# Transposing keys as fp32 words of two bf16, and a query projection in row form, in a decode step that streams 162 MB

## The chip, the cores and the metric

The kernel runs on 1 core of one Trainium2 chip. The metric is the device time of one execution in microseconds (us), given as the median of several runs. The *span* is the time from the first to the last instruction that the profile shows. It is shorter than the device time: 390.4 us of 393.2 us in the profiled run of the kernel before.

Engine names: PE multiplies matrices, PEld is PE's weight load, DVE, ACT and POOL are the vector, scalar and general engines, SP only starts loads here.

## The reference, cut to what matters

One token of one sequence goes through attention over a cache, and through a gated MLP, and a gate mixes the two. Everything is bf16.

```python
# x [1,1,1024]; k_cache, v_cache [1,4,65536,128]; wq [1024,4096]; wo [4096,1024]
g = sigmoid((x * gate_w).sum(-1))
q = x @ wq                                    # 32 query heads of 128, 8 to each key head
p = softmax(q @ k.T * 128 ** -0.5)            # over 65536 keys
a = (p @ v).reshape(1, 1, 4096) @ wo
b = gmlp(x, w_in, w_sp, b_sp, w_out)
return g * a + (1 - g) * b
```

## The kernel before

All large operands pass through one ring of five 4 MB slots. There are 41 loads: 2 of wq, 16 pairs of key units, 16 pairs of value units, 2 of w_in, 1 of w_out, 4 of wo. SP starts load n when the last PE instruction that reads load n−5 has ended. This is the only link from the speed of PE back to the speed of the loads.

```python
# issue(): SP starts load n into slot n % NS (NS = 5); the operation has to wait
# for all readers of the slot. done(key): the last key of load n was used, start n + 5.
P("SP", f, w=[("slot", s)], dma="s%d" % s)
...
# gate: needs gate_w, and is recorded ahead of the query projection
P("DVE", lambda e: e.tensor_tensor(z2[:, 0:KC], xT, gw, ALU.mult), r=["xT", "gw"], w=["z2"])
...
# query projection, column form: 256 matmuls of one column
for k in range(2):
    for h in range(HQ):
        ins = e.matmul(pf(OB)[:, h:h + 1], sl[:, WQ_N * k + 128 * h:WQ_N * k + 128 * (h + 1)],
                       xT[:, 2 * i + k:2 * i + k + 1], ...)
```

A *unit* is 8192 keys of one key head. Keys lie in rows; this kernel's product with the queries reads them in columns, so a unit takes 64 transposes of 128x128, in 8 batches into PSUM, each batch copied out by DVE (5 of 8) or ACT (3 of 8), and then 16 score matmuls.

```python
def tr(e, b=b, pb=pb):                        # one batch of k_piece
    for t in range(8):
        ins = e.transpose(pbf(pb)[:, 128 * t:128 * (t + 1)],
                          sl[:, 128 * (8 * b + t):128 * (8 * b + t + 1)], idb)
...
def f(e):                                     # s_piece, after every two batches
    for cg in range(4):
        src = ktb(first + cg // 2)[:, 512 * (cg % 2):512 * (cg % 2 + 1)]
        ins = e.matmul(pf(SCB)[32 * cg:32 * (cg + 1), :],
                       qpad[:, 128 * g + 32 * j:128 * g + 32 * (j + 1)], src, ...)
```

A matmul or a transpose of bf16 is two PE instructions, a weight load and a multiply: the 2048 key transposes are 2048 of each on the page.

Of the kernel before, what the change touches and what calls it, by code (L numbers as in the profile page):

```python
# [137 lines left out]
def bass_gated_mix__gqa_block_cached__mixer_gmlp__decode_kernel(  # L138
# [28 lines left out]
    NS = 5  # L167
    SLOT = 16384
    NB = TILES // 8
    NKTS = 6  # L170
    NSC = 10
    QW = DO // 4
    SCALE = 1.0 / math.sqrt(Dh)
# [13 lines left out]
    for name, n in [  # L187
        ("RING", NS * SLOT), ("KT", NKTS * 1024), ("SC", NSC * 1024), ("PSB", 1024), ("PTSB", 1024),
        ("QPAD", G * 128), ("IDB", 128), ("IDF", 256), ("BM", 256), ("ONES", 256), ("SEL", 16 * 32),
        ("M16", 32), ("M8", 16), ("M32", 64), ("MQ", 32), ("OT", 256), ("XT", KC), ("GW", KC), ("WB", 2), ("MAXC", 2 * G * NU), ("LP", 2 * G * NU),  # L190
        ("COLS", 2 * 64), ("DM", 32), ("OSB", 1024), ("OSC", 512), ("OV", OC), ("Z", 2 * 28), ("Z2", 2 * 28),
        ("ZG", 2 * 28), ("ZE", 2 * 28), ("YB", FC), ("BROW", 2 * QW), ("OROW", QW),
    ]:
        region(name, n)
# [3 lines left out]
    def ab(name, n, o=0):  # L198
        return arena[:, OFF[name] + o:OFF[name] + o + n]

    def af(name, n, o=0):
        return arena[:, OFF[name] + 2 * o:OFF[name] + 2 * (o + n)].bitcast(F32)
# [11 lines left out]
    maxc, lp, colt = af("MAXC", G * NU), af("LP", G * NU), af("COLS", 64)  # L214
    zc, z2, zg, ze = af("Z", 28), af("Z2", 28), af("ZG", 28), af("ZE", 28)
    yb, ovec, orow, brow = ab("YB", FC), ab("OV", OC), ab("OROW", QW), af("BROW", QW)
    osb, osc, dm = af("OSB", 512), ab("OSC", 512), af("DM", 16)
    col = lambda i: colt[:, i:i + 1]
    (C_GS, C_GE, C_G1, C_G, C_OMG, C_MU, C_V, C_S0, C_R0, C_S1, C_R1, C_AL, C_BE, C_T) = range(14)
    C_G4 = 16  # L220
# [1 line left out]
    def gcol(g, i):  # L222
        return col(C_G4 + 11 * g + i)
# [20 lines left out]
    def B(i):  # L244
        return ("bank", i)
# [7 lines left out]
    P("DVE", lambda e: e.memset(ones, 1.0), w=["ones"])  # L253
    P("DVE", lambda e: e.memset(brow, 0.0), w=["brow"])
    P("DVE", lambda e: e.memset(pf(MB), 0.0), w=[B(MB)])


    def small(dst, src, key):
# [106 lines left out]
      r=["m32"], w=["sel"])  # L365
    P("DVE", lambda e: e.tensor_reduce(mq, vw(idf, 0, [[1, 16], [16, 8]]), AXX, ALU.add), r=["idf"], w=["mq"])


    P("DVE", lambda e: e.tensor_tensor(z2[:, 0:KC], xT, gw, ALU.mult), r=["xT", "gw"], w=["z2"])  # L369
    P("DVE", lambda e: e.tensor_reduce(col(C_GS), z2[:, 0:KC], AXX, ALU.add), r=["z2"], w=["gs"])  # L370
# [6 lines left out]
      r=["g"], w=["omg"])  # L377


    for i in range(4):  # L380
        sl, key = use(("wq", i))

        def f(e, i=i, sl=sl):
            for k in range(2):
                for h in range(HQ):
                    ins = e.matmul(pf(OB)[:, h:h + 1], sl[:, WQ_N * k + 128 * h:WQ_N * k + 128 * (h + 1)],  # L386
                                   xT[:, 2 * i + k:2 * i + k + 1], start=(i == 0 and k == 0 and h == 0),
                                   stop=(i == 3 and k == 1), skip_group_check=True)
            return ins
        P("PE", f, r=["xT", key], w=[B(OB)])  # L390
        done(("wq", i))
    for g in range(G):
        P("DVE", lambda e, g=g: e.tensor_copy(vw(qpad, 128 * g, [[40, 4], [1, 8]]),
                                              vw(pf(OB), 8 * g, [[0, 4], [1, 8]])),
          r=[B(OB)], w=["qpad"])


    nbatch = [0]
    pend = []

    def k_piece(n, j):
        sl, key = use(("k", n))
        first = nbatch[0]
        for b in (2 * j, 2 * j + 1):
            i = nbatch[0]
            nbatch[0] += 1
            pb = KTB[i % 4]

            def tr(e, b=b, pb=pb):
                for t in range(8):  # L410
                    ins = e.transpose(pbf(pb)[:, 128 * t:128 * (t + 1)],  # L411
                                      sl[:, 128 * (8 * b + t):128 * (8 * b + t + 1)], idb)
                return ins
            P("PE", tr, r=["idb", key], w=[B(pb)])
            if b in (2, 5, 7):
                P("ACT", lambda e, i=i, pb=pb: e.activation(ktb(i), pbf(pb), ACTF.Copy),  # L416
                  w=[("kt", i % NKTS), B(pb)])
            else:
                P("DVE", lambda e, i=i, pb=pb: e.tensor_copy(ktb(i), pbf(pb)), w=[("kt", i % NKTS), B(pb)])  # L419
        if j == 3:  # L420
            done(("k", n))
        pend.append((n, j, first))

    def s_piece():
        if not pend:
            return
        n, j, first = pend.pop(0)
        g, u = KV[n]

        def f(e):  # L430
            for cg in range(4):
                src = ktb(first + cg // 2)[:, 512 * (cg % 2):512 * (cg % 2 + 1)]
                ins = e.matmul(pf(SCB)[32 * cg:32 * (cg + 1), :], qpad[:, 128 * g + 32 * j:128 * g + 32 * (j + 1)], src,  # L433
                               start=(j == 0), stop=(j == 3), tile_position=(0, 32 * cg), skip_group_check=True)
            return ins
        P("PE", f, r=["qpad", ("kt", first % NKTS), ("kt", (first + 1) % NKTS)], w=[B(SCB)])
        if j == 3:
            P("DVE", lambda e: e.tensor_scalar(scs(n), pf(SCB), 0.0, None, op0=ALU.add, op1=ALU.max,  # L438
                                               accum_out=maxc[:, n:n + 1]), w=[("sc", n % NSC), ("mx", n), B(SCB)])
            if u == NU - 1:  # L440
                max_piece(g)
# [29 lines left out]
    def pv_piece(n):  # L471
        g, u = KV[n]
        sl, key = use(("v", n))

        def f(e):
            for xi in range(4):
                for cg in range(4):
                    ins = e.matmul(pf(OB)[32 * cg:32 * (cg + 1), :],  # L478
                                   ptsb(n)[:, 128 * xi + 32 * cg:128 * xi + 32 * (cg + 1)],
                                   vw(sl, 128 * (4 * cg + xi), [[2048, 4], [1, 128]]),  # L480
                                   start=(u == 0 and xi == 0), stop=(u == NU - 1 and xi == 3),
                                   tile_position=(0, 32 * cg), skip_group_check=True)
            return ins
        P("PE", f, r=[("ptsb", n % 2), key], w=[B(OB)])
        done(("v", n))
        if u == NU - 1:
            out_piece(g)

    def out_piece(g):
        P("DVE", lambda e: e.tensor_copy(osb, pf(OB)), w=["osb", B(OB)])  # L490
        P("DVE", lambda e: e.tensor_reduce(gcol(g, K_L), lp[:, NU * g:NU * (g + 1)], AXX, ALU.add),
          r=[("lp", NU * g + u) for u in range(NU)], w=[("l", g)])
        P("DVE", lambda e: e.tensor_tensor(gcol(g, K_LW), gcol(g, K_L), gcol(g, K_W), ALU.mult),
# [4 lines left out]
        P("DVE", lambda e: e.scalar_tensor_tensor(gcol(g, K_F), gcol(g, K_RL), gcol(g, K_W), col(C_G),  # L498
                                                  op0=ALU.mult, op1=ALU.mult),
          r=[("rl", g), ("w", g), "g"], w=[("f", g)])  # L500
        P("DVE", lambda e: e.tensor_scalar(osc, osb, gcol(g, K_F), None, op0=ALU.mult),
          r=["osb", ("f", g)], w=["osc"])

        def f(e):
            for c in range(4):
# [86 lines left out]
    for si, (k, v, aux) in enumerate(steps):  # L592
# [4 lines left out]
            start_exp(v)  # L597
        for j in range(4):
            if k is not None:
                k_piece(k, j)  # L600
                s_piece() if len(pend) > 1 else None
            if j == 1 and v is not None:
                pt_piece(v)
            if j == 2 and nxt is not None and (k is not None or not pend):
                start_exp(nxt)
            if j == 3 and v is not None:
                pv_piece(v)
# [53 lines left out]
```

## Time and profile before

| | before |
|---|---|
| device time, median of 3 runs | 392.74 us (392.17 to 393.21) |
| span of the profiled run | 390.4 us (other runs of this kernel: up to 392.9) |
| bytes loaded | 162.01 MB |
| PE busy, and its mean granted clock | 274.1 us, 0.850 |
| PE instructions | 3902 multiplies and 3902 weight loads |

These are lines of the page of the kernel before. The first three give the span, the busy time of each engine, and the rate of the loads in 40 slices of 9.76 us; `q1` is the queue of the loads, `q8` and `q14` are queues of instruction fetches (packets, MB, share of the time of 16 DMA engines); then come the shares of the chain of work that ended last, and two costly groups (busy us, mean ns of one | idle time just before, and what ended it).

```profile
span 390.4 us, 8502 instructions
...
PE 274.1 (70%) x3902; PEld 194.6 (50%) x3902; DVE 160.2 (41%) x347; ACT 124.4 (32%) x171; POOL 1.5 (0%) x8
...
GB/s 322 430 430 437 418 412 441 426 428 425 411 405 431 433 426 431 428 431 428 427 431 428 428 431 430 425 435 435 428 431 433 428 426 431 433 431 421 416 415 96
...
q1 hardware_dynamic: 5912, 162.01, 97.1%
q8 instruction: 30, 0.49, 0.5%
...
q14 instruction: 4, 0.03, 0.0%
...
DMA 55%; PE 36%; DVE 6%; issue 1%; ACT 1%; ACTq 0%; DVEq 0%
...
L411 PE MATMUL pb<-arena 128*128 128x128 bf16 x2048 | 153.6, 235 | 31.7 <-DMA arena<-in_A_k_cache_dram 31.7
L411 PEld LDWEIGHTS pb<-arena 128*128 128x128 bf16 x2048 | 131.9, 106 | 60.1 <-DMA arena<-in_A_k_cache_dram 34.7
```

The loads run at about 430 GB/s almost throughout and their queue fills 97.1% of the time of 16 DMA engines, so the loads set the time. PE, busy 70% of the time, spends it mostly on the 2048 key transposes.

The next lines are the timeline of SP, cut to three loads: the time of an issue, its duration, the engine and the line, and what is loaded. An issue shows when a slot came free. The first two slots are those of wq, the third is a key slot.

```profile
44.99 0.33 SPq L338 DMA_DIRECT2D arena<-in_B_w_in_dram  x1
50.67 0.33 SPq L338 DMA_DIRECT2D arena<-in_A_k_cache_dram  x1
...
106.72 0.33 SPq L338 DMA_DIRECT2D arena<-in_A_k_cache_dram  x1
```

The following stretches show busy time per engine with counts in brackets, granted clock, share of busy DMA and the rate. The first shows a dip to 344 GB/s. The issue at 106.72 us above came when the queue was running dry. (The rate of a stretch counts a packet whole where it starts, so stretches of 2 us scatter by tens of GB/s; this one is of 6 us.) The last three stretches are the end of the stream.

```profile
core 0: us, PE busy (x) PEld busy (x) DVE busy (x) ACT busy (x) POOL busy (x), PEclk, DMA share, GB/s
106.00:112.00 6.00, 5.79 (x91) 4.39 (x89) 4.00 (x8) 3.47 (x4) 0.00 (x0) 1.00 0.88 344
380.00:382.00 2.00, 1.01 (x32) 0.67 (x32) 0.00 (x0) 0.00 (x0) 0.00 (x0) 1.00 0.60 254
382.00:384.00 2.00, 0.04 (x4) 0.00 (x0) 0.00 (x0) 0.00 (x0) 0.00 (x0) 0.54 0.52 221
384.00:386.00 2.00, 0.05 (x4) 0.08 (x8) 0.00 (x0) 0.00 (x0) 0.00 (x0) 0.50 0.17 74
```

The end of the timeline before shows the matmuls of the last wo load and the addition that follows. They start at 385.95 us.

```profile
385.95 1.88 PE L621 MATMUL pb<-arena 128*1 128x256 bf16 x32 [3.91 <-DMA arena<-in_A_wo_dram]
387.88 0.42 DVE L627 TENSOR_TENSOR arena<-pb,arena 97x256 bf16<-97x256 f32 x1 [12.56 <-PE pb L621]
```

### The profile page before, as it was taken

Reading aid. Unit: us, or ns where it says so; the run is one execution under the profiler, and the core shown is the slowest. Engines: PE = TensorE matmul, PEld = TensorE weight load, DVE = VectorE, ACT = ScalarE, POOL = GpSimd, SP = SyncE. Lnnn points to the kernel's source line nnn. Section 1 sums busy time; section 2 is a strip of 40 time slices with the busy share of each in tenths; the row PEclk is TensorE's granted clock in tenths of the full one; section 3 lists DMA queues with packets and bytes.
Section 4 is the critical chain, followed back from the end, with each engine's and each line's share of the span. In section 5 each row is a group of like instructions: output and inputs, shape, how many; then the busy total and the mean of one; then the engine's idle time right before and its main releaser. Section 6 shows DMA issues by size and latency. Waiting matters only on the chain.

```text
span 390.4 us, 8502 instructions
## 1 busy us (share of the span) xinstructions
PE 274.1 (70%) x3902; PEld 194.6 (50%) x3902; DVE 160.2 (41%) x347; ACT 124.4 (32%) x171; POOL 1.5 (0%) x8
## 2 busy tenths in 40 slices
PE   0000699996999899976787596957974959574552
PEld 0000678885776676745565474645743736221121
DVE  2000043435666666644664263536742636410020
ACT  1000033332556555551355151613551425231000
POOL 1000000000000000000000000000000000000000
PEclk9999998685999999996899598968995989856555
DMA  8999999999999999999999999999999999999992
GB/s 322 430 430 437 418 412 441 426 428 425 411 405 431 433 426 431 428 431 428 427 431 428 428 431 430 425 435 435 428 431 433 428 426 431 433 431 421 416 415 96
DMA packets 6778, 162.54 MB, mean 416 GB/s; under 512 B 1492, under 2 KB 1496, under 8 KB 1496
## 3 DMA queue, kind: packets, MB, share of 16 engines
q1 hardware_dynamic: 5912, 162.01, 97.1%
q8 instruction: 30, 0.49, 0.5%
q10 hardware_dynamic: 832, 0.00, 0.1%
q14 instruction: 4, 0.03, 0.0%
HBM read 162.01 MB, written 0.00 MB: 415 GB/s over the span
## 4 chain that ended last, share of the span: by engine, by line
DMA 55%; PE 36%; DVE 6%; issue 1%; ACT 1%; ACTq 0%; DVEq 0%
DMA arena<-in_A_k_cache_dram 31%; PE pb L411 18%; DMA arena<-in_gate_w_dram 10%; DMA arena<-in_A_v_cache_dram 8%; PE pb L433 6%; DMA arena<-in_A_wo_dram 6%; PE pb L526 3%; DVE arena L419 3%; PE pb L478 3%; PE pb L386 2%; DVE arena L438 2%; PE pb L466 1%; ACT arena L416 0%; PE pb L621 0%; PE pb L574 0%
## 5 line engine op out<-in xcount | busy, mean ns | idle before, releaser
L411 PE MATMUL pb<-arena 128*128 128x128 bf16 x2048 | 153.6, 235 | 31.7 <-DMA arena<-in_A_k_cache_dram 31.7
L411 PEld LDWEIGHTS pb<-arena 128*128 128x128 bf16 x2048 | 131.9, 106 | 60.1 <-DMA arena<-in_A_k_cache_dram 34.7
L419 DVE COPY arena<-pb 128x1024 bf16<-128x1024 bf16 x160 | 108.3, 689 | 111.2 <-PE pb L411 110.2
L416 ACT ACTIVATE arena<-pb 128x1024 bf16<-128x1024 bf16 x96 | 98.0, 1021 | 162.2 <-PE pb L411 162.2
L433 PE MATMUL pb<-arena 128*32 128x512 bf16 x512 | 55.0, 420 | 6.1 <-DVE arena L438 4.2
L478 PE MATMUL pb<-arena 128*32 128x512 bf16 x512 | 39.9, 440 | 14.5 <-DMA arena<-in_A_v_cache_dram 10.5
L371 PE MATMUL pb<-arena 128*128 128x1 f32 x2 | 0.6, 362 | 41.0 <-DVE arena L370 41.0
L478 PEld LDWEIGHTS pb<-arena 128*32 128x32 bf16 x512 | 14.0, 104 | 28.5 <-issue 13.5
L459 ACT ACTIVATE arena<-arena 128x512 bf16<-128x512 f32 x32 | 22.8, 713 | 14.3 <-PE pb L466 12.6
L469 DVE COPY arena<-pb 128x512 bf16<-128x512 bf16 x32 | 13.6, 424 | 28.4 <-PE pb L466 28.4
L433 PEld LDWEIGHTS pb<-arena 128*32 128x32 bf16 x512 | 13.3, 93 | 22.9 <-DVE arena L438 7.7
L438 DVE TENSOR_SCALAR_CACHE_REDUCE arena<-pb 128x512 f32<-128x512 f32 x32 | 21.8, 682 | 2.8 <-PE pb L433 2.8
L371 PEld LDWEIGHTS pb<-arena 128*128 128x128 f32 x2 | 0.5, 313 | 41.0 <-DVE arena L370 41.0
L369 DVE TENSOR_TENSOR arena<-arena 128x8 f32<-128x8 bf16 x1 | 0.2, 168 | 37.2 <-DMA arena<-in_gate_w_dram 37.2
L466 PE MATMUL pb<-arena 128*128 128x128 bf16 x128 | 14.8, 248 | 0.0
L466 PEld LDWEIGHTS pb<-arena 128*128 128x128 bf16 x128 | 8.7, 109 | 11.4 <-issue 10.6
L526 PEld LDWEIGHTS pb<-arena 128*128 128x128 bf16 x224 | 13.6, 158 | 0.5 <-issue 0.5
L526 PE MATMUL pb<-arena 128*128 128x1 bf16 x224 | 13.8, 198 | 0.0
L373 ACT ACTIVATE arena<-pb 128x1 f32<-128x1 f32 x1 | 0.2, 171 | 37.0 <-PE pb L371 37.0
L621 PE MATMUL pb<-arena 128*1 128x256 bf16 x128 | 6.5, 379 | 6.8 <-DMA arena<-in_A_wo_dram 6.8
L386 PE MATMUL pb<-arena 128*128 128x1 bf16 x256 | 7.1, 165 | 2.1 <-issue 2.1
L621 PEld LDWEIGHTS pb<-arena 128*1 128x1 bf16 x128 | 3.6, 108 | 9.4 <-issue 4.4
(78 smaller groups left out, 59.7 us busy)
## 6 DMA issues: line engine op xcount, KB each, us to landing
arena<-in_A_k_cache_dram SPq DMA_DIRECT2D x16, 4096.0 KB, 30.2
arena<-in_A_v_cache_dram SPq DMA_DIRECT2D x16, 4096.0 KB, 31.7
arena<-in_A_wq_dram SPq DMA_DIRECT2D x2, 4096.0 KB, 17.4
arena<-in_A_wo_dram SPq DMA_DIRECT2D x4, 2048.0 KB, 30.1
arena<-in_B_w_in_dram SPq DMA_DIRECT2D x2, 3584.0 KB, 28.0
arena<-in_B_w_out_dram SPq DMA_DIRECT2D x1, 3584.0 KB, 17.3
arena<-in_A_x_dram ACTq DMA_DIRECT2D x1, 2.0 KB, 22.4
arena<-in_gate_w_dram ACTq DMA_DIRECT2D x1, 2.0 KB, 39.2
```

Of the source, the lines that this page charges most:

```text
L386: ins = e.matmul(pf(OB)[:, h:h + 1], sl[:, WQ_N * k + 128 * h:WQ_N * k + 128 * (h + 1)], xT[:, 2 * i + k:2 * i + k + 1], start=(i == 0 and ...
L411: ins = e.transpose(pbf(pb)[:, 128 * t:128 * (t + 1)], sl[:, 128 * (8 * b + t):128 * (8 * b + t + 1)], idb)
L416: P("ACT", lambda e, i=i, pb=pb: e.activation(ktb(i), pbf(pb), ACTF.Copy), w=[("kt", i % NKTS), B(pb)])
L419: P("DVE", lambda e, i=i, pb=pb: e.tensor_copy(ktb(i), pbf(pb)), w=[("kt", i % NKTS), B(pb)])
L433: ins = e.matmul(pf(SCB)[32 * cg:32 * (cg + 1), :], qpad[:, 128 * g + 32 * j:128 * g + 32 * (j + 1)], src, start=(j == 0), stop=(j == 3), ...
L438: P("DVE", lambda e: e.tensor_scalar(scs(n), pf(SCB), 0.0, None, op0=ALU.add, op1=ALU.max, accum_out=maxc[:, n:n + 1]), w=[("sc", n % NSC) ...
L459: P("ACT", lambda e: e.activation(psb(n), scs(n), ACTF.Exp, bias=gcol(g, K_NB), scale=SCALE, accum_out=lp[:, n:n + 1]), r=[("sc", n % NSC) ...
L466: ins = e.transpose(pbf(PTB)[:, 128 * xi:128 * (xi + 1)], psb(n)[:, 128 * xi:128 * (xi + 1)], idb)
L469: P("DVE", lambda e: e.tensor_copy(ptsb(n), pbf(PTB)[:, 0:512]), w=[("ptsb", n % 2), B(PTB)])
L478: ins = e.matmul(pf(OB)[32 * cg:32 * (cg + 1), :], ptsb(n)[:, 128 * xi + 32 * cg:128 * xi + 32 * (cg + 1)], vw(sl, 128 * (4 * cg + xi), [[ ...
L526: ins = e.matmul(pf(MB)[:, z:z + 1], vw(sl, c0, [[FC, 128]]), xT[:, 2 * i + k:2 * i + k + 1], start=(i == 0 and k == 0 and z == 0), stop=( ...
L621: ins = e.matmul(pf(FB)[32 * q:32 * q + 1, 0:QW], ovec[:, 8 * i + c:8 * i + c + 1], sl[:, DO * c + QW * q:DO * c + QW * (q + 1)], start=(i ...
```

## The change

The intent is to relieve PE. Two neighbouring bf16 of a key slot are read as one fp32 word. A transpose of 128 such words moves 256 bf16, two keys per partition, so a unit takes 32 transposes where it took 64. The transposed tile then holds the even and odd elements of a key pair interleaved, so the score matmuls read with a stride of 2, with queries arranged to match. The arrangement needs the query projection in row form: 64 matmuls of 512 columns, a transpose of the result and a small selection matmul. A copy in the output stage goes away. The loads, their order and the copies out of PSUM stay. `NKTS` is the number of buffers for transposed tiles, one more than before.

```diff
-    NKTS = 6
+    NKTS = 7
...
+                        ins = e.matmul(pf(OB)[32 * cg:32 * cg + 2, :], xw[:, 3 * c + 1 - s:3 * c + 3 - s],
+                                       sl[:, WQ_N * k + 512 * (4 * s + cg):WQ_N * k + 512 * (4 * s + cg + 1)],
+                                       ...  # 64 of these for 256 of one column; then copy, 4 transposes,
+                                            # copy, 2 selection matmuls, 8 copies into qpad
...
         sl, key = use(("k", n))
+        sl = sl.bitcast(F32)
...
-                for t in range(8):
-                    ins = e.transpose(pbf(pb)[:, 128 * t:128 * (t + 1)],
-                                      sl[:, 128 * (8 * b + t):128 * (8 * b + t + 1)], idb)
+                for t in range(4):
+                    ins = e.transpose(pf(pb)[:, 128 * t:128 * (t + 1)],
+                                      sl[:, 128 * (4 * b + t):128 * (4 * b + t + 1)], idf)
...
+            for ev in range(2):
+                for cg in range(4):
+                    v = 128 * g + 32 * (2 * c + ev)
+                    ins = e.matmul(pf(SCB)[32 * cg:32 * (cg + 1), :], qpad[:, v:v + 32],
+                                   vw(ktb(first + cg), ev, [[2, 512]]), ...)
...
-                                   vw(sl, 128 * (4 * cg + xi), [[2048, 4], [1, 128]]),
+                                   vw(sl, 128 * (8 * cg + 2 * xi), [[4096, 2], [1, 256]]),
...
-        P("DVE", lambda e: e.tensor_copy(osb, pf(OB)), w=["osb", B(OB)])
```

More of the change, by code (lines that the diff above doesn't have):

```diff
@@ L190, in bass_gated_mix__gqa_block_cached__mixer_gmlp__decode_kernel @@
         ("M16", 32), ("M8", 16), ("M32", 64), ("MQ", 32), ("OT", 256), ("XT", KC), ("GW", KC), ("WB", 2), ("MAXC", 2 * G * NU), ("LP", 2 * G * NU),
-        ("COLS", 2 * 64), ("DM", 32), ("OSB", 1024), ("OSC", 512), ("OV", OC), ("Z", 2 * 28), ("Z2", 2 * 28),
+        ("COLS", 2 * 64), ("DM", 32), ("QT", 32), ("XW", 3 * KC), ("SELE", 256), ("OSC", 512), ("OV", OC), ("Z", 2 * 28), ("Z2", 2 * 28),
         ("ZG", 2 * 28), ("ZE", 2 * 28), ("YB", FC), ("BROW", 2 * QW), ("OROW", QW),
@@ L216, in bass_gated_mix__gqa_block_cached__mixer_gmlp__decode_kernel @@
     yb, ovec, orow, brow = ab("YB", FC), ab("OV", OC), ab("OROW", QW), af("BROW", QW)
-    osb, osc, dm = af("OSB", 512), ab("OSC", 512), af("DM", 16)
+    osc, dm = ab("OSC", 512), af("DM", 16)
+    qsb, qT, xw = ab("PSB", 512), ab("QT", 32), ab("XW", 3 * KC)
     col = lambda i: colt[:, i:i + 1]
@@ L255, in bass_gated_mix__gqa_block_cached__mixer_gmlp__decode_kernel @@
     P("DVE", lambda e: e.memset(pf(MB), 0.0), w=[B(MB)])
+    P("DVE", lambda e: e.memset(pf(OB), 0.0), w=[B(OB)])
+    P("DVE", lambda e: e.memset(xw, 0.0), w=["xw"])
     def small(dst, src, key):
@@ L366, in bass_gated_mix__gqa_block_cached__mixer_gmlp__decode_kernel @@
     P("DVE", lambda e: e.tensor_reduce(mq, vw(idf, 0, [[1, 16], [16, 8]]), AXX, ALU.add), r=["idf"], w=["mq"])
+    for ev in range(2):
+        P("DVE", lambda e, ev=ev: e.tensor_copy(vw(ab("SELE", 128, 128 * ev), 0, [[64, 2], [1, 64]]),
+                                                vw(idb, ev, [[0, 2], [2, 64]])), r=["idb"], w=["sele"])
     P("DVE", lambda e: e.tensor_tensor(z2[:, 0:KC], xT, gw, ALU.mult), r=["xT", "gw"], w=["z2"])
@@ L377, in bass_gated_mix__gqa_block_cached__mixer_gmlp__decode_kernel @@
       r=["g"], w=["omg"])
+    P("DVE", lambda e: e.tensor_copy(vw(xw, 1, [[3, KC]]), xT), r=["xT"], w=["xw"])
     for i in range(4):
@@ L384, in f @@
             for k in range(2):
-                for h in range(HQ):
-                    ins = e.matmul(pf(OB)[:, h:h + 1], sl[:, WQ_N * k + 128 * h:WQ_N * k + 128 * (h + 1)],
-                                   xT[:, 2 * i + k:2 * i + k + 1], start=(i == 0 and k == 0 and h == 0),
-                                   stop=(i == 3 and k == 1), skip_group_check=True)
+                c = 2 * i + k
+                for s in range(2):
+                    for cg in range(4):
+                        ins = e.matmul(pf(OB)[32 * cg:32 * cg + 2, :], xw[:, 3 * c + 1 - s:3 * c + 3 - s],
+                                       sl[:, WQ_N * k + 512 * (4 * s + cg):WQ_N * k + 512 * (4 * s + cg + 1)],
+                                       start=(c == 0 and s == 0), stop=(c == KC - 1 and s == 1),
+                                       tile_position=(0, 32 * cg), skip_group_check=True)
             return ins
-        P("PE", f, r=["xT", key], w=[B(OB)])
+        P("PE", f, r=["xw", key], w=[B(OB)])
         done(("wq", i))
+    P("DVE", lambda e: e.tensor_copy(qsb[0:98, :], pf(OB)[0:98, :]), w=[("psb", 0), B(OB)])
+    def f(e):
+        for c in range(4):
+            ins = e.transpose(pbf(PTB)[:, 128 * c:128 * c + 98], qsb[0:98, 128 * c:128 * (c + 1)], idb[0:98, 0:98])
+        return ins
+    P("PE", f, r=[("psb", 0), "idb"], w=[B(PTB)])
+    P("DVE", lambda e: e.tensor_copy(vw(qT, 0, [[16, 2], [4, 4], [1, 4]]),
+                                     vw(pbf(PTB), 0, [[1, 2], [32, 4], [128, 4]])), w=["qT", B(PTB)])
+    def f(e):
+        for ev in range(2):
+            ins = e.matmul(pf(PTB)[:, 32 * ev:32 * (ev + 1)], ab("SELE", 128, 128 * ev), qT, start=True, stop=True)
+        return ins
+    P("PE", f, r=["sele", "qT"], w=[B(PTB)])
     for g in range(G):
-        P("DVE", lambda e, g=g: e.tensor_copy(vw(qpad, 128 * g, [[40, 4], [1, 8]]),
-                                              vw(pf(OB), 8 * g, [[0, 4], [1, 8]])),
-          r=[B(OB)], w=["qpad"])
+        for par in range(2):
+            P("DVE", lambda e, g=g, par=par: e.tensor_copy(
+                vw(qpad, 128 * g + 8 * par, [[80, 2], [32, 2], [1, 8]], 64 * par, 64),
+                vw(pf(PTB), 8 * g, [[0, 2], [32, 2], [1, 8]], 64 * par, 64)), r=[B(PTB)], w=["qpad"])
     nbatch = [0]
@@ L402, in k_piece @@
         sl, key = use(("k", n))
-        first = nbatch[0]
+        sl = sl.bitcast(F32)
         for b in (2 * j, 2 * j + 1):
@@ L409, in tr @@
             def tr(e, b=b, pb=pb):
-                for t in range(8):
-                    ins = e.transpose(pbf(pb)[:, 128 * t:128 * (t + 1)],
-                                      sl[:, 128 * (8 * b + t):128 * (8 * b + t + 1)], idb)
+                for t in range(4):
+                    ins = e.transpose(pf(pb)[:, 128 * t:128 * (t + 1)],
+                                      sl[:, 128 * (4 * b + t):128 * (4 * b + t + 1)], idf)
                 return ins
-            P("PE", tr, r=["idb", key], w=[B(pb)])
+            P("PE", tr, r=["idf", key], w=[B(pb)])
             if b in (2, 5, 7):
@@ L421, in k_piece @@
             done(("k", n))
-        pend.append((n, j, first))
+        if j % 2 == 1:
+            pend.append((n, j // 2, nbatch[0] - 4))
     def s_piece():
@@ L426, in s_piece @@
             return
-        n, j, first = pend.pop(0)
+        n, c, first = pend.pop(0)
         g, u = KV[n]
         def f(e):
-            for cg in range(4):
-                src = ktb(first + cg // 2)[:, 512 * (cg % 2):512 * (cg % 2 + 1)]
-                ins = e.matmul(pf(SCB)[32 * cg:32 * (cg + 1), :], qpad[:, 128 * g + 32 * j:128 * g + 32 * (j + 1)], src,
-                               start=(j == 0), stop=(j == 3), tile_position=(0, 32 * cg), skip_group_check=True)
-            return ins
-        P("PE", f, r=["qpad", ("kt", first % NKTS), ("kt", (first + 1) % NKTS)], w=[B(SCB)])
-        if j == 3:
+            for ev in range(2):
+                for cg in range(4):
+                    v = 128 * g + 32 * (2 * c + ev)
+                    ins = e.matmul(pf(SCB)[32 * cg:32 * (cg + 1), :], qpad[:, v:v + 32],
+                                   vw(ktb(first + cg), ev, [[2, 512]]), start=(c == 0 and ev == 0),
+                                   stop=(c == 1 and ev == 1), tile_position=(0, 32 * cg), skip_group_check=True)
+            return ins
+        P("PE", f, r=["qpad"] + [("kt", (first + i) % NKTS) for i in range(4)], w=[B(SCB)])
+        if c == 1:
             P("DVE", lambda e: e.tensor_scalar(scs(n), pf(SCB), 0.0, None, op0=ALU.add, op1=ALU.max,
@@ L500, in out_piece @@
           r=[("rl", g), ("w", g), "g"], w=[("f", g)])
-        P("DVE", lambda e: e.tensor_scalar(osc, osb, gcol(g, K_F), None, op0=ALU.mult),
-          r=["osb", ("f", g)], w=["osc"])
+        P("DVE", lambda e: e.tensor_scalar(osc, pf(OB), gcol(g, K_F), None, op0=ALU.mult),
+          r=[("f", g)], w=["osc", B(OB)])
         def f(e):
@@ L599, in bass_gated_mix__gqa_block_cached__mixer_gmlp__decode_kernel @@
             if k is not None:
+                ready = len(pend)
                 k_piece(k, j)
-                s_piece() if len(pend) > 1 else None
+                s_piece() if ready else None
             if j == 1 and v is not None:
```

## The prediction

> **What bounds the kernel now.** The load queue. The DMA rows of the page read 0.9 in nearly every slice and 425 to 435 GB/s; 162 MB at 429 GB/s is 378 us of a 390 us span. The rest: the start and 4.4 us from the landing of the last wo piece (385.95) to the end. From 173 us on PE idles 5 us and more at a time for K and V (chain of waits). PE sets the pace only in one stretch: gate_w lands at 40 us, so PE starts at 41 us with five ring slots full and works off a backlog until about 150 us. There a key unit takes 5.6 us against 4.9 us of DMA, slots come free late, and the rate sags once: a slot is released at 106.7 us, when by my count the queue ran dry near 104.5 us; 106 to 112 us shows 328 to 360 GB/s (windows). That costs 1 to 2 us, all a faster PE can win.
>
> **What the change does.** Bytes and order of loads stay.
> - 2048 bf16 key transposes (16 in 1.00 us at full clock) become 1024 of fp32. fp32 weight loads of other lines take 187 ns against 98 for bf16, each with about 85 that one column costs; I estimate 105 ns of occupancy. [...] 105 to 125 ns each, 3.4 to 4.0 us per unit where 4.0 stand now. No fp32 transpose is in the trace.
> - Evictions stay (DVE 0.69 us, ACT 1.02). Scores: the same 16 matmuls per unit, now stride 2; I expect the same 0.33 to 0.40 us per four. The stall of about 2 us per unit on the score eviction should shrink. A key unit goes from 5.6 to about 5 us, a key and value step from 6.7 to 6.0 to 6.5.
> - Query projection: 256 one-column matmuls (9.1 us with a 2.1 us stall) become 64 of 512 columns, four side by side: about 6 us, plus 3 us of copies and small matmuls, and a start 1 us later. A wash.
> - The output stage loses a 0.69 us copy, four times; hidden.
>
> **On the critical path:** only the sag at 106 us, 0 to 2 us. The rest becomes DMA waits.
>
> **Time:** 391.6 us, 8 in 10 between 389.0 and 395.5. Faster by over 2%: 2%; within 2%: 89%; slower by over 2%: 9%.
>
> **What would show it.** DMA still 425 to 435 GB/s; 1024 transposes, eight in 0.85 to 1.0 us at full clock; a K and V step under 6.7 us; no dip at 106 to 112 us; PE busy below 274 us, mean granted clock below 0.85; the last wo piece at 384 to 386 us, 4.4 us before the end.
>
> **What would make it wrong.** A dearer fp32 transpose. Working the ring through with the trace's durations, I estimate: a key unit 1 us longer (transpose at 155 ns) costs 4 to 6 us in all, 2 us longer (190 ns) 13 to 15 us, slots coming free late; 215 ns would make PE the bound at about 410 us. Strided key reads that double the score matmuls (1.3 us per unit) would do the same. A gain over 2% needs a faster DMA rate.

One passage is cut from it, where marked: the grounds on which the fp32 transpose was taken to go in one pass bound by its weight load. The 105 to 125 ns of a transpose stand as the author's estimate, from the 187, 98 and 85 ns, and the sum comes to 391.6 us: the 392.74 us of the kernel before, less 1.1 us out of the 0 to 2 put on the sag.

## More of the kernel before

The whole program is unrolled: no instruction is executed twice.

## The result, and the profile after

| | before | after |
|---|---|---|
| device time, median of 4 runs each | 392.98 us (392.17 to 393.64) | 390.62 us (390.55 to 390.83) |
| span of the profiled run | 390.4 us | 389.0 us |
| mean granted clock | 0.850 | 0.852 |
| PE instructions | 7804 | 5384 |
| instruction fetches in the span | 30 | 21 |
| start of the last wo matmuls | 385.95 us | 384.54 us |

The ratio of after to before is 0.9942, with an interval of 0.9922 to 0.9962, so the kernel is the same within 2% but 2.3 us faster. Ratios in this document are the mean time of one kernel's fast runs over that of the other's of the same rounds, so they are not quite the ratio of the medians in the tables.

These are the lines of the page after that answer to those of before (its line of `q14` is the same).

```profile
span 389.0 us, 6080 instructions
...
PE 267.3 (69%) x2692; PEld 181.6 (47%) x2692; DVE 159.7 (41%) x354; ACT 124.3 (32%) x171; POOL 1.5 (0%) x8
...
GB/s 324 431 431 438 415 397 445 440 432 426 431 426 426 424 426 438 430 431 424 430 431 430 431 426 431 430 431 430 433 431 430 429 430 431 430 431 423 428 414 83
...
q1 hardware_dynamic: 5912, 162.01, 97.3%
q8 instruction: 21, 0.34, 0.4%
...
DMA 62%; PE 33%; DVE 3%; ACT 1%; issue 1%; ACTq 0%; DVEq 0%
...
L440 PE MATMUL pb<-arena 128*128 128x128 f32 x1024 | 155.5, 304 | 39.5 <-DMA arena<-in_A_k_cache_dram 38.9
L440 PEld LDWEIGHTS pb<-arena 128*128 128x128 f32 x1024 | 127.7, 157 | 80.3 <-DMA arena<-in_A_k_cache_dram 42.5
```

PE has lost 1210 multiplies and as many weight loads, but only 7 us of busy time: a transpose of fp32 costs more than one of bf16 (304 ns against 235 as the page has it: durations of overlapping instructions, at all granted clocks). The chain leans more on the loads, 62% against 55%. The rate is what it was.

The cost of one fp32 transpose can be read where PE does nothing else. These are four lines of the timeline after, two stretches of 16 transposes each, the first at half clock and the second at full clock (0.50 and 1.00 granted in these stretches): start, duration, engine.

```profile
69.02 3.28 PEld L440 LDWEIGHTS pb<-arena 128*128 128x128 f32 x16 [0.84 <-issue]
69.02 3.56 PE L440 MATMUL pb<-arena 128*128 128x128 f32 x16
...
73.09 1.73 PEld L440 LDWEIGHTS pb<-arena 128*128 128x128 f32 x16 [0.45 <-issue]
73.10 1.97 PE L440 MATMUL pb<-arena 128*128 128x128 f32 x16
```

At full clock 16 weight loads take 1.73 us, 108 ns each; at half clock 3.28 us, 205 ns each. So an fp32 transpose is one weight load and one multiply (1024 transposes are 1024 of each on the page), and its pace went by the granted clock: 205 ns at 0.50, 108 ns at 1.00. Loads and multiplies both follow one another at 109 ns, so the trace doesn't tell which of the two sets the pace.

The slots, in the timeline of SP after, are freed earlier: the second wq slot at 47.30 us for 50.67, the key slot at 103.69 for 106.72.

```profile
45.58 0.33 SPq L341 DMA_DIRECT2D arena<-in_B_w_in_dram  x1
47.30 0.33 SPq L341 DMA_DIRECT2D arena<-in_A_k_cache_dram  x1
...
103.69 0.33 SPq L341 DMA_DIRECT2D arena<-in_A_k_cache_dram  x1
```

The dip is gone (423 GB/s over the 6 us that showed 344), and the end of the stream has moved.

```profile
106.00:112.00 6.00, 6.00 (x101) 4.36 (x99) 2.92 (x7) 3.45 (x4) 0.00 (x0) 1.00 0.99 423
380.00:382.00 2.00, 1.47 (x28) 0.65 (x20) 0.00 (x0) 0.00 (x0) 0.00 (x0) 0.50 0.52 221
382.00:384.00 2.00, 0.00 (x0) 0.00 (x0) 0.00 (x0) 0.00 (x0) 0.00 (x0) 0.50 0.21 90
384.00:386.00 2.00, 1.46 (x31) 0.97 (x32) 0.00 (x0) 0.00 (x0) 0.00 (x0) 0.50 0.00 0
```

```profile
384.54 1.88 PE L653 MATMUL pb<-arena 128*1 128x256 bf16 x32 [3.08 <-DMA arena<-in_A_wo_dram]
386.47 0.43 DVE L659 TENSOR_TENSOR arena<-pb,arena 97x256 bf16<-97x256 f32 x1 [14.06 <-PE pb L653]
```

The last matmuls start 1.4 us earlier, 384.54 for 385.95. From there the two kernels take the same time to the end (4.4 us). So the gain is in the stream of loads. The three last stretches show something that the sum of the prediction had no place for: in both kernels the rate falls by steps at the end, 254, 221, 74 GB/s before and 221, 90, 0 after. The 16 DMA engines do not finish together: by the DMA records they end the last load between 380.3 and 385.4 us before, and between 378.8 and 384.0 us after.

### The profile page after: what moved, and what is told of

It reads as the page before. It is cut to its first block, busy times and chain, and to the rows that moved or that the text cites. A ratio compares the mean times of both kernels' runs of the same rounds, so it can differ in the third digit from the quotient of the medians.

```text
span 389.0 us, 6080 instructions
## 1 busy us (share of the span) xinstructions
PE 267.3 (69%) x2692; PEld 181.6 (47%) x2692; DVE 159.7 (41%) x354; ACT 124.3 (32%) x171; POOL 1.5 (0%) x8
## 2 busy tenths in 40 slices
DMA packets 6769, 162.39 MB, mean 418 GB/s; under 512 B 1492, under 2 KB 1496, under 8 KB 1496
## 4 chain that ended last, share of the span: by engine, by line
DMA 62%; PE 33%; DVE 3%; ACT 1%; issue 1%; ACTq 0%; DVEq 0%
DMA arena<-in_A_k_cache_dram 38%; PE pb L440 18%; DMA arena<-in_gate_w_dram 10%; DMA arena<-in_A_v_cache_dram 8%; DMA arena<-in_A_wo_dram 6%; PE pb L464 5%; PE pb L557 3%; PE pb L510 3%; PE pb L396 1%; DVE arena L448 1%; PE pb L498 1%; ACT arena L445 0%; PE pb L653 0%; PE pb L605 0%; DVE arena L421 0%
## 5 line engine op out<-in xcount | busy, mean ns | idle before, releaser
L440 PE MATMUL pb<-arena 128*128 128x128 f32 x1024 | 155.5, 304 | 39.5 <-DMA arena<-in_A_k_cache_dram 38.9
L440 PEld LDWEIGHTS pb<-arena 128*128 128x128 f32 x1024 | 127.7, 157 | 80.3 <-DMA arena<-in_A_k_cache_dram 42.5
L510 PE MATMUL pb<-arena 128*32 128x512 bf16 x512 | 39.0, 432 | 15.9 <-DMA arena<-in_A_v_cache_dram 11.7
L464 PE MATMUL pb<-arena 128*32 128x512 bf16 x512 | 45.1, 431 | 3.6 <-ACT arena L445 1.9
L491 ACT ACTIVATE arena<-arena 128x512 bf16<-128x512 f32 x32 | 22.8, 714 | 15.4 <-PE pb L498 13.5
L510 PEld LDWEIGHTS pb<-arena 128*32 128x32 bf16 x512 | 11.7, 102 | 30.9 <-issue 19.8
L378 PEld LDWEIGHTS pb<-arena 128*128 128x128 f32 x2 | 0.5, 313 | 40.8 <-DVE arena L377 40.8
L464 PEld LDWEIGHTS pb<-arena 128*32 128x32 bf16 x512 | 8.3, 96 | 16.9 <-issue 8.4
L498 PE MATMUL pb<-arena 128*128 128x128 bf16 x128 | 15.3, 255 | 0.0
L498 PEld LDWEIGHTS pb<-arena 128*128 128x128 bf16 x128 | 11.5, 117 | 5.7 <-issue 4.2
L557 PEld LDWEIGHTS pb<-arena 128*128 128x128 bf16 x224 | 13.7, 159 | 0.0
L557 PE MATMUL pb<-arena 128*128 128x1 bf16 x224 | 13.7, 198 | 0.0
## 6 DMA issues: line engine op xcount, KB each, us to landing
arena<-in_A_wo_dram SPq DMA_DIRECT2D x4, 2048.0 KB, 30.5
```

The lines of the kernel that those rows point to most:

```text
L440: ins = e.transpose(pf(pb)[:, 128 * t:128 * (t + 1)], sl[:, 128 * (4 * b + t):128 * (4 * b + t + 1)], idf)
L464: ins = e.matmul(pf(SCB)[32 * cg:32 * (cg + 1), :], qpad[:, v:v + 32], vw(ktb(first + cg), ev, [[2, 512]]), start=(c == 0 and ev == 0), st ...
L491: P("ACT", lambda e: e.activation(psb(n), scs(n), ACTF.Exp, bias=gcol(g, K_NB), scale=SCALE, accum_out=lp[:, n:n + 1]), r=[("sc", n % NSC) ...
L498: ins = e.transpose(pbf(PTB)[:, 128 * xi:128 * (xi + 1)], psb(n)[:, 128 * xi:128 * (xi + 1)], idb)
L510: ins = e.matmul(pf(OB)[32 * cg:32 * (cg + 1), :], ptsb(n)[:, 128 * xi + 32 * cg:128 * xi + 32 * (cg + 1)], vw(sl, 128 * (8 * cg + 2 * xi) ...
L557: ins = e.matmul(pf(MB)[:, z:z + 1], vw(sl, c0, [[FC, 128]]), xT[:, 2 * i + k:2 * i + k + 1], start=(i == 0 and k == 0 and z == 0), stop=( ...
```

## The experiments

Twelve kernels ran, all within the tolerance of the reference. Each ratio is against runs of the kernel before on the same chip in the same rounds (its medians there: 393.14, 392.99, 393.20 and 392.67 us, 11 runs each).

### First question: which part of the change brings the 2.3 us?

The theories were these. A: the query stage frees the ring earlier, so that the backlog never empties the queue. B: the words do it, by faster key units. The names are those used in the expectations.

**e1_rows**: the kernel before, with only the query projection in row form.

```diff
-                    ins = e.matmul(pf(OB)[:, h:h + 1], sl[:, ... 128 * h ...], xT[:, ...], ...)   # 256
+                        ins = e.matmul(pf(OB)[32 * cg:32 * cg + 2, :], xw[:, ...], sl[:, ... 512 ...], ...)   # 64
+    P("DVE", lambda e: e.tensor_copy(qsb[0:98, :], pf(OB)[0:98, :]), w=[("psb", 0), B(OB)])
+    ...  # 4 transposes, then a copy into qT; no even and odd halves
```

> The kernel before with the query projection in row form alone; keys stay bf16. Theory A (the query stage makes the gain): the trace of after has the slot that the load queue needed near 104.5 us free 3.0 us sooner (103.7 for 106.7), and already the wq slot 3.4 us sooner (47.3 for 50.7), so this kernel alone should free that slot at 103 to 104 us, lose the dip of the rate at 106 to 110 us, and land the last wo piece about 1.4 us sooner (384.5): span 389.0, ratio to before 0.994 to 0.997. Rival B (the fp32 key transposes make it): slot still free at about 106 us, dip still there, span 390.4, ratio 1.000. The 1.0 us of the gain that lies outside the span (393.2 less 390.4 before, 390.8 less 389.0 after): if it goes with the instruction count (8502 to 6080) this kernel, with about 8130, keeps 2.7 us of it; if it is a fetch of instructions after the last work (before shows one at 392.2 us, after none), it can fall either way and the trace must show that fetch when it is 2.8 us.

Measured: 392.09 us (391.84 to 392.17), ratio 0.9968 (0.9949 to 0.9986), span 390.0. The second wq slot came free at 47.41 us and the key slot at 101.69, earlier than in the kernel after (103.69).

**e2_words**: the kernel after, with the query projection back in column form.

```diff
-                        ins = e.matmul(pf(OB)[32 * cg:32 * cg + 2, :], xw[:, ...], sl[:, ... 512 ...], ...)   # 64
+                    ins = e.matmul(pf(OB)[:, h:h + 1], sl[:, ... 128 * h ...], xT[:, ...], ...)   # 256
...
+    P("DVE", lambda e: e.tensor_copy(qT, pf(OB)[:, 0:32]), w=["qT", B(OB)])
```

> The change without its row-form query: keys transposed as fp32 words, query projected in columns as before. Theory A: no gain in the span; the query stage ends at 50.6 us, plus 2 us of the copies that spread it over even and odd elements, so the slot comes free at 106 to 108 us, the dip of the rate stays, the last wo piece lands at 385.5 to 387 us, span 390 to 391.5, ratio 0.997 to 1.003. Rival B: slot free at about 104 us, span 389.0, ratio 0.994. Time outside the span: 1.8 us if it follows the instruction count (about 6460).

Measured: 391.28 us (390.50 to 391.65), ratio 0.9945 (0.9927 to 0.9964), span 388.7. The key slot came free at 105.28 us.

What follows: theory A falls. The query stage alone frees the ring earliest and gains least; the words alone free it late and have nearly the whole gain. B got the part right and the way wrong: its slot came later than B said, and the gain was there all the same. So the time at which that slot comes free doesn't explain the gain.

### Second question: what is the dry moment worth?

In both kernels PE cannot start before 41 us, because the gate computation waits for gate_w, which lands at 40 us. Moving its recording to the place where the gate is first needed lets PE start at 22.8 us. Then the backlog never builds, and there can be no dry moment.

**e3_gate**: the kernel before with that move; **e4_gate_after**: the kernel after with the same move.

```diff
-    P("DVE", lambda e: e.tensor_tensor(z2[:, 0:KC], xT, gw, ALU.mult), r=["xT", "gw"], w=["z2"])
-    ...  # 7 operations of the gate, ahead of the query projection
 def mixer_piece():
+        P("DVE", lambda e: e.tensor_tensor(z2[:, 0:KC], xT, gw, ALU.mult), r=["xT", "gw"], w=["z2"])
+        ...  # the same 7
```

> The kernel before with the gate's reduction moved from ahead of the query projection to the start of the mixer, so that PE no longer waits for gate_w (40 us) but starts when x and wq are there (22 us). No byte and no instruction is taken away. If the only thing that PE speed could win is the load queue's dry moments, those at 44 to 50 us (about 0.8 us lost) and 106 to 110 us (about 1.4 us) both go: last wo piece at 383.5 to 384, span 388.0 to 388.8, ratio 0.993 to 0.996. If backlog is not what made the dips: span 390.4, ratio 1.000.

> The changed kernel with the gate's reduction moved the same way. Only the dip at 44 to 50 us is left in it to win: span 388.0 to 388.6, 0.4 to 0.9 us below after, ratio to before 0.991 to 0.993. If the early start also finds fp32 transposes worth something once PE isn't behind: more than 1 us below after. If the two gate kernels have the same span, the key words are worth nothing once the queue never runs dry.

Measured: e3_gate 392.37 us (392.02 to 393.31), ratio 0.9979 (0.9959 to 0.9999), span 390.3. e4_gate_after 390.53 us (390.44 to 390.80), ratio 0.9932 (0.9911 to 0.9953), span 388.6.

The stretch of the dip in e3_gate, and the start of its last matmuls:

```profile
106.00:112.00 6.00, 4.55 (x69) 3.31 (x66) 4.24 (x10) 4.85 (x6) 0.00 (x0) 1.00 0.99 426
```

```profile
385.89 1.88 PE L621 MATMUL pb<-arena 128*1 128x256 bf16 x32 [3.06 <-DMA arena<-in_A_wo_dram]
```

The rate stands at 426 GB/s where it was 344, the key slot came free at 91.15 us instead of 106.72, and the last load lands where it did: matmuls at 385.89 for 385.95. The median of the spans falls from 391.0 to 390.4 us, about 0.6 us, and they scatter less: 390.2 to 390.6, where those of the kernel before go from 390.4 to 392.4. This is what the dry moment is worth in these rounds; against the medians of the kernel before in the other rounds (390.7 to 391.4) it would be 0.3 to 1.0. The expectation of e3_gate (span 388.0 to 388.8) was missed. It had also taken the low rate at 44 to 50 us for a dry moment; that stays, at 340 to 375 GB/s from 43 to 47 us by the DMA records, although slots came free at 26 and 32 us in e3_gate, so the loads were not waiting for PE there. Its cause is open. And the kernel after, which has no dry moment, gains nothing from an even earlier start (388.6 in the profiled run, against 388.5 to 389.0). Some 1.6 us of the gain remain, between two kernels that both keep the queue full.

### Third question: what is left?

With the queue never dry and the same bytes, what still ends 1.6 us earlier? The packets of the load queue go at the same pace in both kernels: in the trace's own DMA records a 32 KB packet takes 1.214 to 1.216 us on one engine in the median of every run. But the engines do not keep together. Each load ends with one record of four bytes from each of the 16 engines, and these records show how late each engine is. This is a reckoning from the DMA records of the traces, not a view of the profile. For the 36th of the 41 loads, at about 350 us (us behind the first engine, sorted):

```
kernel     fetches so far   lag of the 16 engines
e7_fewer   16   0  0 .1 .1 .3 .5 .8 3.0 3.2 3.2 3.2 3.2 3.4 3.4 3.4 3.6
after      19   0 .1 .1 .1 .2 .6 .9 3.2 3.3 3.4 3.4 3.4 3.4 4.8 4.9 5.3
e3_gate    29   0  0 .1 .1 .2 .3 .8 3.1 4.6 4.7 4.9 6.3 6.3 6.4 6.5 6.7
e6_pad13   31   0  0 .1 .1 .2 .4 .8 3.1 4.8 6.2 6.3 6.3 6.4 6.4 6.5 6.5
```

(e6_pad13 and e7_fewer are from the runs below.) Seven engines are on time, one is 3.1 us late whatever the kernel, and eight are late in steps of about 1.6 us. The number of steps adds up to the number of *instruction fetches*, spread evenly over those eight engines: after, 19 = 5x2 + 3x3; e3_gate, 29 = 3x3 + 5x4. The kernel before is not in the table, since its dry moment let late engines catch up: at the 11th load eight of its engines are 1.2 to 1.9 us late, and at the 12th, after the dry moment, 15 of the 16 are within 0.8 us.

How the lags come about can be watched within one run. In e3_gate, at the 3rd to the 8th load, when 1, 2, 3, 4, 5 and 6 fetches have been made, exactly 1, 2, 3, 4, 5 and 6 engines are 1.5 to 1.9 us behind, and all others are within 0.4 us. The engine that is 3.1 us late whatever the kernel fits the other queue of instruction fetches: `q14` has four packets of 8 KB in the span of every run. In e3_gate they come at 79, 120, 190 and 322 us; one engine falls back by about 1 us, and so to 1.1, 2.1 and 3.1 us, at the loads after the first, the third and the fourth of them, and another falls back to 0.7 us after the second. In the kernel after it is the same at 73, 132, 176 and 306 us.

Theory C is drawn from this. Before e5_pad10, e6_pad13 and e7_fewer ran, it said that each block of fetched instructions puts one of the 16 DMA engines 1.2 us behind; the eight engines, the 1.6 us and the staircase below were read off only with these three runs. In its final form, each block holds up one of eight DMA engines by about 1.6 us. PE has 2420 instructions less; a fetch is a packet of 16,384 bytes and, by the counts, 256 instructions (7804/256 = 30.5, 5384/256 = 21.0; the page lists 30 and 21). The last matmuls of every run in the table at the end of this question start 0.55 to 0.62 us after the slowest engine is done with their load, so they waited for the slowest. By theory C, then, the fetches put off the last landing. If they are dealt out to the eight engines in turn, the last landing should even be a staircase: 378.7 us, at which the first engine ends in all kernels without a dry moment, and 1.6 us for each *started eight* of fetches.

What a fetch costs at the end of the stream, the following runs measure.

**e5_pad10**: the kernel after, with 2424 one-column weight loads added, whose result nobody uses. They bring the fetches back to the number of the kernel before. They can't slow the stream by making PE late: a step with keys and values takes PE 6.29 us in the kernel after, and the 4 MB of keys and values that it needs take 9.75 us to load.

```diff
+        if v is not None:
+            def idle(e, m=105 if k is not None else 1):
+                for _ in range(m):
+                    ins = e.ldweights(idb[:, 0:1])
+                return ins
+            P("PE", idle, r=["idb"])
         if v is not None and v % NU == 0:
             weight_piece(v // NU)
```

**e6_pad13**: the same with 120 of them in steps with keys and values and 60 in steps with values alone, 3300 in all.

```diff
+            def idle(e, m=120 if k is not None else 60):
```

**e7_fewer**: the kernel after with half of the score matmuls and half of the value matmuls left out, for fewer instructions. It computes something wrong; the outputs are so small that it passed the tolerance all the same.

```diff
+                    if ev != c:
+                        continue
...
-            for xi in range(4):
+            for xi in (0, 3):
```

> The changed kernel with 2424 weight loads of one column added on PE (105 after each of the 23 key-and-value steps, in time that PE spends waiting for loads, and one after each value step). They bring its instruction fetches from 21 back to about 31, as the kernel before has; nothing else changes. Theory C (what the first four runs left: every fetch of 16 KB that PE's instruction stream needs puts one of the 16 DMA engines 1.2 us behind, the last load lands when the slowest engine is done, and the fp32 keys gain because they are 2048 instructions fewer): the gap between the first and the last engine at the last load grows from 5.2 to about 6 to 6.5 us, while the first engine still ends at 378.8; span 389.7 to 390.6 (e1_rows 390.0 to 390.4 and e3_gate 390.2 to 390.6 had 29 and 31 fetches), time 391.6 to 392.5. Rival D (fewer instructions don't matter; the gain is faster key work, or transposes of another kind that disturb the loads less): span 388.6 to 389.2, time 390.6.

> The same with 120 such loads per key-and-value step and 60 per value step, about 3300 in all: about 34 fetches. Theory C: 0 to 0.7 us over e5_pad10 (span 390.0 to 391.2). Rival D: span 388.6 to 389.2. A key-and-value step should stay under the 9.75 us of its loads (about 6.3 plus 3 us); if it does not, the first engine's end moves from 378.8 and the run tells nothing.

> Wrong result on purpose: the changed kernel with half of its score matmuls and half of its value matmuls left out, 1024 PE instructions fewer, about 17 fetches. Theory C: slowest engine about 0.3 to 1 us less behind, span 388.0 to 388.7, time 389.8 to 390.5. Rival D: span 388.6 to 389.0, since the queue doesn't run dry in the changed kernel either way.

**after_again** is the kernel after, unchanged, in the same rounds.

> The changed kernel unchanged, on the same chip and in the same rounds as the three above, as their base: span 388.6 to 389.2, time 390.5 to 391.2, 21 fetches, gap between the first and the last engine near 5 us.

Measured: e5_pad10 392.08 us (391.99 to 392.25), ratio 0.9971 (0.9954 to 0.9988); e6_pad13 393.61 us (393.51 to 393.81), ratio 1.0010 (0.9993 to 1.0027); e7_fewer 390.42 us (390.14 to 390.61), ratio 0.9928 (0.9910 to 0.9945); after_again 390.58 us (390.33 to 390.77), ratio 0.9933 (0.9914 to 0.9952). These lines of e6_pad13 are of its page and of the end of its timeline. PE then spent 7.75 us per step with keys and values (138.13 to 145.88 us), of the 9.75 us that its loads take, so it was never what the loads waited for.

```profile
span 391.8 us, 9380 instructions
...
q8 instruction: 34, 0.56, 0.6%
```

```profile
387.32 1.87 PE L659 MATMUL pb<-arena 128*1 128x256 bf16 x32 [3.08 <-DMA arena<-in_A_wo_dram]
```

Instructions that do nothing, on an engine that has time to spare, cost 1.5 us, and then 3.0 us: the whole of the gain and more is given back. By theory C as first put, e6_pad13 should have stayed within 391.2; at 391.8 it missed that. e5_pad10 lies where e3_gate lies (spans 390.3 and 390.3), though its PE does the words. But four kernels do not tell a staircase from a straight line. e7_fewer hints at stairs: 17 fetches or 21, nearly the same time.

**e8_pad3** and **e9_pad6** decide this: 561 and 1389 of the same loads, 23 and 26 fetches, on either side of 24. The cost per fetch of e5_pad10 and e6_pad13, drawn as a straight line (1.5 us for 9 fetches, 3.0 for 13), would put e9_pad6 0.5 to 0.7 us above e8_pad3; stairs put it 1.6 above.

```diff
+            def idle(e, m=24 if k is not None else 1):     # e8_pad3
+            def idle(e, m=60 if k is not None else 1):     # e9_pad6
```

> A sharper test of theory C. When the 16 engines complete each load, their lags in all ten traces fall into two groups: eight engines that are late by whole steps of about 1.6 us, and eight that are not (one of them by 3.1 us, the same in all kernels). With n fetches of PE instructions done, n mod 8 of the late ones have one step more: after 19 fetches 5 engines at 3.3 us and 3 at 4.8, after 29 (e3_gate) 3 at 4.7 and 5 at 6.4. So I take it that fetches go around eight engines in turn, and the last load lands at 378.8 us plus about 1.6 us for each started eight: a staircase. This kernel has 561 added weight loads, 23 or 24 fetches. Staircase: no step over after: span 388.5 to 389.1, last load landed by 384.1. A straight line through 21 fetches (388.7) and 34 (391.8), 0.24 us each, would give 389.2 to 389.5.

> The same with 1389 added weight loads, 26 or 27 fetches. Staircase: one whole step over e8_pad3 and as much as e5_pad10 with its 30: span 389.8 to 390.4, last load landed at 384.8 to 385.4. Straight line: 389.9 to 390.2. It is the pair that decides: staircase 1.2 to 1.6 us between the two, line 0.6 to 0.8 us.

Measured: e8_pad3 390.55 us (390.45 to 390.61), ratio 0.9937 (0.9922 to 0.9951); e9_pad6 392.16 us (391.96 to 392.85), ratio 0.9980 (0.9963 to 0.9997). Page and end of the timeline of e8_pad3, then of e9_pad6:

```profile
span 388.6 us, 6641 instructions
...
q8 instruction: 23, 0.38, 0.4%
```

```profile
384.23 1.88 PE L659 MATMUL pb<-arena 128*1 128x256 bf16 x32 [3.08 <-DMA arena<-in_A_wo_dram]
```

```profile
span 390.2 us, 7469 instructions
...
q8 instruction: 26, 0.43, 0.4%
```

```profile
385.72 1.88 PE L659 MATMUL pb<-arena 128*1 128x256 bf16 x32 [3.08 <-DMA arena<-in_A_wo_dram]
```

561 instructions more cost nothing, 828 more on top of these cost 1.5 us, and another 1035 (e5_pad10) nothing. That is the staircase. It also rules out that the added weight loads disturb the stream by themselves, since that would grow with their number. All profiled runs side by side; the landing is reckoned from the DMA records like the lags above, the stair is 378.7 + 1.6 x (fetches/8, rounded up):

| kernel | fetches | stair, us | last landing, us | span, median of its runs |
|---|---|---|---|---|
| e7_fewer | 17 | 383.5 | 383.3 | 388.6 |
| after, after_again | 21, 21 | 383.5 | 384.0, 383.6 | 388.8, 388.75 |
| e4_gate_after | 21 | 383.5 | 383.7 | 388.7 |
| e2_words | 23 | 383.5 | 383.7 | 388.85 |
| e8_pad3 | 23 | 383.5 | 383.7 | 388.75 |
| e9_pad6 | 26 | 385.1 | 385.1 | 390.2 |
| e1_rows | 29 | 385.1 | 385.0 | 390.2 |
| e5_pad10 | 30 | 385.1 | 385.3 | 390.25 |
| e3_gate | 31 | 385.1 | 385.3 | 390.4 |
| e6_pad13 | 34 | 386.7 | 386.7 | 391.8 |
| before, with a dry moment | 30 | – | 385.4 | 390.7 to 391.4 |

(The last fetch of e2_words and of e3_gate comes after the last landing; their stairs are the same without it.) The stairs were read off the runs up to e7_fewer; e8_pad3 and e9_pad6 were run to test them, and met them. The table also tells where the two halves of the change fall: e2_words, with 23 fetches, is on the low stair and e1_rows, with 29, on the high one, which is what the first question had asked.

### A trial that told nothing

If the eight late engines are known, the last load could be shared out so that late engines get less. **e10_split2** and **e11_split4** try it on the kernel after: the last wo load of 128 rows is split into 112 rows and two transfers of 8 rows, and into 96 rows and four of 8. Each small transfer ends with eight records of four bytes: the traces have 16 and 32 packets under 512 bytes more than that of the kernel after (1508 and 1524 for 1492). So each was taken to go to eight engines; which they are, no run here shows. What the expectations assumed of it is cut from them, where marked: "those" and "they" below are the engines of the small transfers, and the first case of e11_split4 is that they are the punctual ones. A gain or a loss of about 0.6 us (an estimate from the 0.615 us of a 16 KB packet of a load) was to tell whether they are the late ones.

```diff
+            top = 128 - 8 * 2 if keys[0] == ("wo", 3) else 128       # 8 * 4 in e11_split4
-                    ins = e.dma_start(slot(n)[:, c0:c0 + src.shape[1]], src)
+                    ins = e.dma_start(slot(n)[0:top, c0:c0 + src.shape[1]], src[0:top, :])
+            for j in range((128 - top) // 8):
+                p0, src = top + 8 * j, pieces[0][1]
+                P("SP", lambda e, n=n, p0=p0, src=src: e.dma_start(slot(n)[p0:p0 + 8, 0:src.shape[1]],
+                                                                   src[p0:p0 + 8, :]), w=[("wx", j)], dma="wx%d" % j)
```

> A try to use the finding: the changed kernel, with 16 of the 128 rows of the last wo piece taken out of its transfer and sent as two transfers of 8 rows each. [...] If those are the eight that instruction fetches don't delay, the eight late ones carry 16 KB (0.6 us) less in the end: last load at about 383.1, span 388.0 to 388.4. If they are the late ones: 0.6 us later, span 389.2 to 389.6. No change (388.7) would mean that the small transfers don't go where I think.

> The same with 32 rows in four transfers. [...] the late ones carry 32 KB (1.2 us) less, but the one engine that is 3.1 us late in every kernel, fetches or not, carries 1.2 us more, so 388.0 to 388.5, no better than e10_split2. If they are the late ones: 1.2 us later, span 389.8 to 390.2.

Measured: 396.40 us (396.16 to 397.11), ratio 1.0089 (1.0072 to 1.0106), and 397.34 us (397.11 to 397.40), ratio 1.0113 (1.0096 to 1.0131). Both missed all expectations by far. From 375 to 381 us all 16 engines were busy, but the rate was 218 and 202 GB/s; a 16 KB packet that started after 374 us took 1.11 and 1.18 us in the mean, where 0.615 is usual, and up to 1.9. The cause is open. The runs say nothing of which engines are late, and which eight they are stays open too.

## Why the prediction was right or wrong

The time was predicted at 391.6 us and came out at 390.62, within the range and within 2%. The main reason held: 162 MB at 430 GB/s set the time, and PE is not what it waits for.

What held in detail:
- The fp32 transpose is one weight load and one multiply (1024 of each on the page for 1024 transposes; the four fp32 matmuls of L483 are 8 of each in the same trace), and takes 108 ns at full clock, where 105 to 125 was predicted, eight in 0.86 us. That the weight load sets the pace is not shown. At full clock one such load lasts 138 to 142 ns here, where a bf16 one lasts 95 to 99, and they follow one another at 109 ns for 56.
- A step with keys and values takes 6.29 us (two of them from 135.67 to 148.24), under the 6.7 predicted as a bound.
- The dip is gone, PE is busy for 267 us, less than 274, and the last wo matmuls start at 384.5 us, in the predicted 384 to 386, 4.4 us before the end.

What was wrong:
- "That costs 1 to 2 us, all a faster PE can win." The dry moment is worth about 0.6 us (e3_gate). In the profiled run it is worth less still: the last landing is the same with it and without it (385.4 and 385.3), because this dry moment also let the late engines catch up (eight of them 1.2 to 1.9 us late before it, one after it). That last part is read from one profiled run, and a short one: of 44 runs of the kernel before, 14 have a span within the 390.6 us that e3_gate keeps to, and the profiled one is like these.
- "**On the critical path:** only the sag at 106 us, 0 to 2 us." This is the step that failed. The larger part, about 1.6 us, was a term that the sum did not have: 2420 fewer PE instructions are 9 fewer fetches of 256, and the slowest DMA engine is held up by three fetches instead of four. It was shown by adding the instructions back without their work (e5_pad10, e9_pad6). With 1.6 taken as the difference of e3_gate and after (390.4 to 388.8), the two make up the 2.2 us between the median spans of before (391.0) and after by construction; e5_pad10, with 1.5 us over after_again, measures the second part by itself. So that the total came near the prediction was in the larger part luck: the reason was another than the one given.
- "Query projection: ... A wash." It frees its ring slot 3.4 us sooner (47.30 for 50.67). Alone it gives 0.8 us of span (391.0 to 390.2, e1_rows), about what the removal of the dry moment gives, since its key slot comes free at 101.69 us; on top of the words it gives nothing that the spans show (388.85 without it, 388.8 with it).
- "A key unit goes from 5.6 to about 5 us." It went to 5.4 at full clock (97.17 to 102.56 us). The fp32 transpose was rightly sized, but there was less to win: 32 of them take 3.5 us, and 64 of bf16 had taken 3.6 in the same stretch of the kernel before (16 in 0.90 us from 100.02 us on), not 4.0.
- "Mean granted clock below 0.85." It was 0.852, where it had been 0.850, with PE busy for 267.3 us, where it had been 274.1.

Of the theories formed after the result, A (the query stage) fell with e1_rows and e2_words, and B (faster key units, through the time of the slot) fell in its mechanism. An idea in the first expectations, that the time outside of the span goes with the number of instructions, fell as well: that rest is 1.75 to 2.92 us in kernels with many instructions and with few. What stays open: why a fetch of 16 KB holds up an engine by 1.6 us, when its packet lasts about 1.05 us and 16 KB of a load take 0.61; which eight engines are meant, and why those of `q14` seem to hold up other engines, by 0.7 to about 1 us each; and what slowed the split loads. That `q14` makes the one engine 3.1 us late is read from the times of its packets, and no experiment changed it.

## What to carry to other kernels

Here, by the lags, the instructions of a long unrolled program travelled over the same DMA engines as the loads that bound it, and the last matmuls started 0.55 to 0.62 us after the slowest of them was done: nine fetches were worth 1.6 us of 390. In such a kernel count instruction fetches, and not only the bytes and busy times of engines off the critical path. Look at how far apart the DMA engines finish; padding with harmless instructions on an engine with time to spare is a clean test of whether their number costs anything. And a dip in the rate that goes away with a change is not yet the gain: remove the dip alone and see what is left.
